# A gated linear recurrence by quotients of running products, with the weights converted beside the first feed-forward block

## The chip, the cores and the metric

The kernel runs on one core of a Trainium2 chip. The metric is the device time in microseconds of one execution. A profile of one execution stands beside the times; its span runs from the first to the last instruction.

## The reference

Four batches, 8 heads, 768 tokens, heads of 48 channels; then a bilinear feed-forward layer over the 3072 tokens of 8 x 48 = 384 channels, with 1536 inner columns. The three weights come as float64, all other inputs as float32.

```python
f = 1 / (1 + exp(-f_logit))                       # (B, H, S, D), f_logit = 2 + 0.5 * normal
for t in range(S):
    state = f[t, :, None] * state + k[t, :, None] * v[t, None, :]
    y[t] = q[t] @ state
x = y as (B*S, H*D)                               # 3072 x 384
out = ((x @ w_a) * (x @ w_b)) @ w_out             # 384 -> 1536 -> 384
```

## The kernel before

Two heads share a tile of 128 partitions, one from partition 0, one from partition 64, with channels on partitions and tokens along the free axis. There are 16 such pairs, each with all 768 tokens. `attention` (L135) treats a pair in chunks of 128 tokens. Inside a chunk the scores are made level by level: at level m, a power of two, key and query lie in neighbouring blocks of m tokens, q scaled by the product of f from the start of its block, k by the product to the end of its own. The fine levels (diagonal, 1, 2, 4, 8, 16) are 48 x 32 x 32 matmuls (L175), masked on DVE (L188) and summed on POOL (L195 to L203). Between levels `grow` (L166) multiplies q and k in place on DVE; POOL makes the block products (L156). Levels 32 (L224) and 64 (L243) follow, then transposes of k (L261), the chunks' gains (L271), the chain of states on DVE (L285), and the output (L295 within a chunk, L304 from the state). The six fine levels alone are 288 small matmuls of a pair.

Finished rows of y go by DMA from SP's queue into `xT` (L319), the feed-forward part's input with channels on partitions. `ffn` (L324) takes a batch in two blocks of 384 tokens. A block has 12 steps of six matmuls 128 x 128 x 384 (L335; first b, then a; ACT copies b at L343, DVE multiplies at L345) and 3 steps of 12 matmuls with `w_out` (L350; ACT copies at L358, SP stores at L360).

The weights are converted from float64 by integer operations (`from_double`, L110 to L131) in 36 pieces of 128 x 384: ACT takes the absolute value of the high words (L122), POOL clamps (L123), DVE does four steps (L124 to L127), POOL adds the low words' part (L128), DVE puts the sign back (L129). Three raw buffers hold pieces that are being loaded.

The order of the work is written out: `manual_schedule` keeps each engine's instructions in program order. Two pairs run in turns, and between their groups stands the feed-forward part of the batch before, or, during batch 0, the weights:

```python
            behind = ffn(b - 1) if b else weights()
            n_behind = NB * (NFT + NTG) if b else 3 * NKT * DFF // PIECE
```

So no feed-forward matmul comes ahead of the end of batch 0's recurrence, and the last batch's feed-forward part runs alone.

Of the kernel before, what the change touches and what calls it, by code (L numbers as in the profile page):

```python
# [9 lines left out]
FP32 = mybir.dt.float32  # L10
U32 = mybir.dt.uint32
# [8 lines left out]
R = 64  # partitions that a head takes in a tile of two heads  # L20
# [10 lines left out]
def kernel(  # L31
    ctx: ExitStack,
    tc: tile.TileContext,
    q: bass.AP,  # (B, H, D, S)
    k: bass.AP,  # (B, H, D, S)
    f_logit: bass.AP,  # (B, H, D, S)
    v: bass.AP,  # (B, H/2, C, S/C, 2, D)
    masks: bass.AP,  # (128, len(FINE), 32)
    moe_w_a: bass.AP,  # float32, or float64 as uint64
# [4 lines left out]
    nc = tc.nc  # L44
    B, H, D, S = q.shape
    NCH = S // C
    HP = H // 2
    DFF, DM = moe_w_out.shape[0], out.shape[1]
    NKT, NFT = DM // 128, DFF // 128
# [4 lines left out]
    NSET = 4  # L54

    const = ctx.enter_context(tc.tile_pool(name="const", bufs=1))
    sb2 = ctx.enter_context(tc.tile_pool(name="sb2", bufs=2))
    ab_pool = ctx.enter_context(tc.tile_pool(name="ab", bufs=NFT + 2))
    raw_pool = ctx.enter_context(tc.tile_pool(name="raw", bufs=3))
# [3 lines left out]
    def fixed(shape, name):  # L63
        return const.tile(shape, FP32, tag=name, name=name)
# [302 lines left out]
    with tc.manual_schedule():  # L367
        for i in range(NSET):
            clear_set(i)
            load_pair(i)  # L370
            if i == 0:
                nc.sync.dma_start(out=mask, in_=masks)
                make_identity(nc, ident)
# [60 lines left out]
```

## Time and profile before

| | |
|---|---|
| three runs | 1057.3, 1058.38, 1060.23 us; median 1058.38 |
| profiled execution: span | 1053.9 us, 28435 instructions (its own time is given by this span alone) |
| PE, matmul | busy 814.0 us (77%), 13040 instructions |
| PEld, weight load | busy 517.2 us (49%), 13040 |
| DVE | busy 402.9 us (38%), 780 |
| ACT | busy 141.4 us (13%), 269 |
| POOL | busy 266.3 us (25%), 330 |
| mean granted TensorE clock | 0.891 |
| DMA | 44.39 MB, 42055 packets |

PE is TensorE's matmuls, PEld its weight loads, which run beside them; DVE is VectorE, ACT ScalarE, POOL GpSimd, SP the engine whose queue issues most DMAs. A row of groups gives line, engine, operation, output <- inputs, shapes, count | busy time, mean ns of one | idle time of that engine just before them and what ended it. A row of the timeline gives start and length in us. A row of busy time by stretch gives the stretch, its length, busy time and instructions of PE, PEld, DVE, ACT and POOL, the granted clock, the DMA engines' share and GB/s. An f32 matmul appears as two instructions.

### The profile page before, as it was taken

To read this page: it belongs to the slowest core of one execution; us is meant where nothing else is said; L and a number is where in the kernel's file an instruction comes from. 1 tells how busy PE (TensorE), PEld (TensorE's weight loads), DVE (VectorE), ACT (ScalarE), POOL (GpSimd) and SP (SyncE) were. 2 spreads that over 40 slices of the span, in tenths; PEclk is the share of its full clock that TensorE was granted. 3 is DMA by queue.
4 is the path that set the end of the run, shared out by engine and by line. 5 is a ranking of instruction groups with operands and counts; after the bars stand their busy time and mean duration, and the time that the engine had idled before them with its cause. 6 is when DMAs were issued, how large, how long until landed. Compare 5 with 4: busy or idle time off the path is not lost.

```text
span 1053.9 us, 28435 instructions
## 1 busy us (share of the span) xinstructions
PE 814.0 (77%) x13040; PEld 517.2 (49%) x13040; DVE 402.9 (38%) x780; ACT 141.4 (13%) x269; POOL 266.3 (25%) x330
## 2 busy tenths in 40 slices
PE   2113512125399989997999899979997999999998
PEld 2112312123265656654665566655565656555554
DVE  4556446564445224522452245234523442010110
ACT  1102110120002110201020102010211121110110
POOL 6354144531414031403140314031403140000000
PEclk9999555555599989998999899989998999999999
DMA  9322342224200230032003200320000000000000
GB/s 183 100 58 72 87 117 63 62 75 92 53 3 2 64 74 3 2 72 66 3 2 72 66 3 2 72 66 2 3 20 28 3 2 19 27 1 14 9 1 22
DMA packets 42055, 44.39 MB, mean 42 GB/s; under 512 B 27984, under 2 KB 31184, under 8 KB 41936
## 3 DMA queue, kind: packets, MB, share of 16 engines
q1 hardware_dynamic: 41936, 42.58, 16.7%
q8 instruction: 102, 1.67, 0.7%
q14 instruction: 17, 0.14, 0.0%
HBM read 33.13 MB, written 4.72 MB: 36 GB/s over the span
## 4 chain that ended last, share of the span: by engine, by line
PE 71%; DVE 11%; POOL 8%; issue 4%; DMA 3%; SPq 2%; ACT 1%; DVEq 0%; ACTq 0%; POOLq 0%
PE f L335 38%; PE f L350 18%; PE a L175 6%; PE a L304 3%; PE a L295 3%; POOL h L128 3%; POOL at L203 2%; DVE qg L147 1%; DVE r L127 1%; DVE k_in L166 1%; DVE tmp L188 1%; DVE r L125 1%; DMA raw<-in_moe_w_out_dram 1%; SPq L92 1%; DMA raw<-in_moe_w_a_dram 1%
## 5 line engine op out<-in xcount | busy, mean ns | idle before, releaser
L335 PE MATMUL f<-xT,w_b 128*128 128x384 f32 x576 | 220.2, 521 | 0.0
L335 PE MATMUL f<-xT,w_a 128*128 128x384 f32 x576 | 203.6, 490 | 0.0
L175 PE MATMUL a<-qg,k_in 48*32 48x32 f32 x7680 | 86.9, 216 | 142.4 <-DVE qg L147 63.2
L350 PE MATMUL f<-w_out,ab 128*128 128x384 f32 x576 | 189.7, 487 | 0.0
L345 DVE TENSOR_TENSOR ab<-f,b_sb 128x384 f32<-128x384 f32 x96 | 53.4, 556 | 317.7 <-PE f L335 317.7
L175 PEld LDWEIGHTS a<-qg,k_in 48*32 48x32 f32 x7680 | 77.9, 117 | 166.5 <-issue 70.5
L335 PEld LDWEIGHTS f<-xT,w_a 128*128 128x128 f32 x576 | 111.5, 194 | 79.3 <-issue 5.5
L350 PEld LDWEIGHTS f<-w_out,ab 128*128 128x128 f32 x576 | 108.0, 190 | 71.9
L335 PEld LDWEIGHTS f<-xT,w_b 128*128 128x128 f32 x576 | 108.6, 199 | 64.3 <-issue 7.8
L343 ACT COPY b_sb<-f 128x384 f32<-128x384 f32 x96 | 45.9, 478 | 372.4 <-PE f L335 372.4
L166 DVE TENSOR_TENSOR k_in<-k_in,tots 128x384 f32<-128x384 f32 x96 | 85.4, 890 | 0.0
L197 POOL TENSOR_TENSOR acc<-acc,tmp 128x384 f32<-128x384 f32 x32 | 38.7, 1211 | 176.3 <-DVE tmp L188 175.7
L156 POOL TENSOR_TENSOR tots<-f_in 128x384 f32<-128x384 f32 x16 | 18.1, 1129 | 252.9 <-ACT f_in L145 252.9
L203 POOL TENSOR_TENSOR at<-acc,tmp 32x384 f32<-32x384 f32 x64 | 71.8, 1122 | 4.1
L147 DVE TENSOR_TENSOR qg<-q_in,f_in 128x768 f32<-128x768 f32 x16 | 18.4, 1149 | 140.0 <-ACT f_in L145 139.8
L188 DVE TENSOR_TENSOR tmp<-a,mask 128x384 f32<-128x384 f32 x96 | 48.9, 550 | 42.0 <-PE a L175 40.4
L166 DVE TENSOR_TENSOR qg<-qg,tots 128x384 f32<-128x384 f32 x96 | 61.2, 637 | 9.1 <-PE a L175 7.7
L128 POOL TENSOR_TENSOR h<-h,r 128x384 f32<-128x384 f32 x36 | 35.7, 992 | 95.3 <-DVE r L127 95.3
L295 PE MATMUL a<-at,v_in 128*64 128x128 f32 x384 | 44.6, 331 | 19.3 <-DVE state L285 19.3
L304 PE MATMUL a<-qg,state 128*128 128x128 f32 x160 | 45.2, 370 | 0.0
L122 ACT ACTIVATE h<-raw 128x384 f32<-128x384 f32 x36 | 19.7, 551 | 149.7 <-DMA raw<-in_moe_w_a_dram 51.4
L295 PEld LDWEIGHTS a<-at,v_in 128*64 128x64 f32 x384 | 22.2, 154 | 35.9 <-issue 30.1
(45 smaller groups left out, 504.2 us busy)
## 6 DMA issues: line engine op xcount, KB each, us to landing
f_in<-in_f_logit_dram SPq DMA_DIRECT2D x32, 144.0 KB, 2.8
q_in<-in_q_dram SPq DMA_DIRECT2D x32, 144.0 KB, 3.5
k_in<-in_k_dram SPq DMA_DIRECT2D x32, 144.0 KB, 3.7
v_in<-in_v_dram SPq DMA_DIRECT2D x16, 288.0 KB, 4.8
raw<-in_moe_w_b_dram SPq DMA_DIRECT2D x12, 384.0 KB, 3.1
raw<-in_moe_w_a_dram SPq DMA_DIRECT2D x12, 384.0 KB, 3.2
raw<-in_moe_w_out_dram SPq DMA_DIRECT2D x12, 384.0 KB, 3.0
out_dram<-o_sb SPq DMA_DIRECT2D x24, 192.0 KB, 1.9
```

What stands on the lines that cost most here:

```text
L128: nc.gpsimd.tensor_tensor(h, h, r, ALU.add)
L166: nc.vector.tensor_tensor(x, x, sp[:, :, e:e + 1].broadcast_to((128, nb, m)), ALU.mult)
L175: nc.tensor.matmul(ps[32 * p:32 * p + 32, par, o:o + 32], lhsT=kg[r, s0:s0 + 32], rhs=qs[r, s0:s0 + 32], start=True, stop=True,)
L188: nc.vector.tensor_tensor(tmp[:, par * NCH:(par + 1) * NCH].rearrange("s c l t -> s c (l t)"), ps[:, par, 0:NCH * 64].rearrange("s (c x) - ...
L197: nc.gpsimd.tensor_tensor(acc, acc, tmp[:, :, 0], ALU.add)
L203: nc.gpsimd.tensor_tensor(at[r].rearrange("s two c t -> s (two c) t")[:, :, r], acc[r], tmp[r, :, 1], ALU.add)
L295: nc.tensor.matmul(o[R * par:R * par + R], lhsT=vv[:, c, par], rhs=at[:, par, c], start=True, stop=c == 0, skip_group_check=True,)
L304: nc.tensor.matmul(o, lhsT=st[:, c - 1], rhs=qg[:, c * C:c * C + C], start=False, stop=True, skip_group_check=True)
L335: nc.tensor.matmul(ps[nm], lhsT=w[:, kt, ft * 128:ft * 128 + 128], rhs=x[:, kt, cols], start=kt == 0, stop=kt == NKT - 1,)
L343: nc.scalar.copy(b_sb, ps["b"])
L345: nc.vector.tensor_tensor(ab[ft], ps["a"], b_sb, ALU.mult)
L350: nc.tensor.matmul(o, lhsT=ab[ft][:, tg * 128:tg * 128 + 128], rhs=w_out[:, ft], start=ft == 0, stop=ft == NFT - 1,)
```

## The change

The recurrence now goes in units of 384 tokens of four heads (two head pairs side by side in the free axis): 16 units, two for each of the eight feed-forward blocks. With P_t the running product of f inside a unit, the score of s and t is (q_t P_t) . (k_s / P_s), so no levels are needed. P starts from e^34, which keeps P and 1/P within float32 as long as the product over a unit is not below e^-68.

- `front`: two sigmoids give f and nearly 1/f; POOL and a third ACT pass make a correction factor; two scans on DVE give P, two more 1/P; q and k are multiplied by them in place.
- `scores`: 24 matmuls 48 x 64 x 64 inside sub-blocks of 64 tokens, masked by one DVE operation. `turn`: 6 transposes of k and an ACT copy. `gains`: 24 matmuls (20 in the last half), then the states are running sums on DVE, with one multiplication by P at the unit's end. `within` and `across`: 24 matmuls each into one accumulator, three ACT copies, five DMAs to `xT` from ACT's queue (they were SP's).
- PSUM: one two-bank tile for scores, transposes and gains, one for the output, four banks for the feed-forward part.
- Weights: 36 pieces in the order in which the first block needs them, converted during the start and the first block. `from_double` takes the sign by a Sign activation and puts it back by a product; the absolute value is taken a second time after POOL's sum. ACT has three operations a piece (before one), DVE four (before five), POOL two.
- The order: units 0 and 1 with the first pieces written out by hand; then the parts of each later unit's `slot` at given steps of the feed-forward blocks. In block 0 the conversions stand ahead of each step, and the `w_out` part runs over all three token groups at once.
- A check: DVE notes for each channel and unit whether the product stayed above e^-68; before the last block the notes are summed into one flag. At the end each engine reads the flag, and only if it is set the old scheme runs again over everything (`by_levels`, the old code without the weights).

```diff
+K_EXP = 75.0
+MIDDLE = 34.0
+DECAY_MAX = 68.0
...
+    make_identity(nc, ident)
+    with ExitStack() as pools:
+        by_quotients(pools, tc, q, k, f_logit, v, moe_w_a, moe_w_b, moe_w_out, out, ident, weights, bad)
+    again = nc.values_load(bad[0:1, 0:1], min_val=0, max_val=1, skip_runtime_bounds_check_because="it is a comparison's result")
+    with tc.If(again > 0), ExitStack() as pools:
+        by_levels(pools, tc, q, k, f_logit, v, masks, out, ident, weights)
...
+    def pieces():
+        for ft in range(NFT):
+            for dst, src in ((w_b, moe_w_b), (w_a, moe_w_a)):
+                cols = slice(ft * 128, ft * 128 + 128)
+                yield dst[:, :, cols], src.rearrange("(kt p) c -> p kt c", p=128)[:, :, cols], (NKT, 128)
+        for ft in range(NFT):
+            yield w_out[:, ft:ft + 1], moe_w_out[ft * 128:ft * 128 + 128].unsqueeze(1), (1, DM)
+    todo, raws = list(pieces()), []
+    def load_weights():
+        if len(raws) < len(todo):
+            dst, src, shape = todo[len(raws)]
+            raw = dst
+            if src.dtype != FP32:
+                raw = raw_pool.tile([128, *shape], mybir.dt.uint64, tag="raw", name="raw")
+            nc.sync.dma_start(out=raw, in_=src)
+            raws.append(raw)
+    def convert(n):
+        while done[0] < min(n, len(todo)):
+            dst, src, shape = todo[done[0]]
+            if src.dtype != FP32:
+                from_double(dst, raws[done[0]], shape)
+            done[0] += 1
+            load_weights()
+    def from_double(dst, raw, shape):
+        words = raw.bitcast(U32).rearrange("p k (n two) -> p (k n) two", two=2)
+        lo, hi = words[:, :, 0], words[:, :, 1]
+        h, r, sign = (sb2.tile([128, PIECE], FP32, tag=n, name=n) for n in ("h", "r", "sign"))
+        hu, ru = h.bitcast(U32), r.bitcast(U32)
+        nc.scalar.activation(h, hi.bitcast(FP32), AF.Abs)
+        nc.scalar.activation(sign, hi.bitcast(FP32), AF.Sign)
+        nc.gpsimd.tensor_scalar(h, h, HI_MAX, HI_MIN, ALU.min, ALU.max)
+        nc.vector.tensor_scalar(hu, hu, 3, 0x40000000, ALU.logical_shift_left, ALU.bitwise_xor)
+        nc.vector.tensor_scalar(ru, hu, 0xFF800000, None, ALU.bitwise_and)
+        nc.vector.scalar_tensor_tensor(out=r, in0=lo, scalar=2.0**-52, in1=r, op0=ALU.mult, op1=ALU.mult)
+        nc.gpsimd.tensor_tensor(h, h, r, ALU.add)
+        nc.scalar.activation(h, h, AF.Abs)
+        h, sign = (x.rearrange("p (k n) -> p k n", k=shape[0]) for x in (h, sign))
+        nc.vector.tensor_tensor(dst, h, sign, ALU.mult)
...
+    def front(u):
+        t = sets[u % NSET]
+        x = halves(t["f"])
+        f, inv, fix = (sb2.tile([128, 2 * BLK], FP32, tag=n, name=n) for n in ("f", "inv", "fix"))
+        nc.scalar.activation(f, x, AF.Sigmoid)
+        nc.scalar.activation(inv, x, AF.Sigmoid, bias=less, scale=-1.0)
+        nc.gpsimd.tensor_scalar(inv, inv, math.exp(K_EXP), 1.0, ALU.mult, ALU.add)
+        nc.gpsimd.tensor_tensor(fix, f, inv, ALU.mult)
+        nc.scalar.activation(fix, fix, AF.Identity, bias=two, scale=-1.0)
+        yield
+        for n in range(2):
+            c = slice(n * BLK, n * BLK + BLK)
+            nc.vector.tensor_tensor_scan(x[:, c], f[:, c], zeros, math.exp(MIDDLE), ALU.mult, ALU.add)
+        nc.vector.tensor_scalar(held[:, u], t["f"][:, :, BLK - 1], math.exp(MIDDLE - DECAY_MAX), None, ALU.is_ge)
+        nc.vector.tensor_tensor(halves(t["q"]), halves(t["q"]), x, ALU.mult)
+        yield
+        for n in range(2):
+            c = slice(n * BLK, n * BLK + BLK)
+            nc.vector.tensor_tensor_scan(inv[:, c], inv[:, c], fix[:, c], math.exp(-MIDDLE), ALU.mult, ALU.mult)
+        nc.vector.tensor_tensor(halves(t["k"]), halves(t["k"]), inv, ALU.mult)
+        live[u] = {}
+        yield
+    ps_x, ps_y = (ps_a.tile([128, 2, 512], FP32, tag=n, name=n) for n in ("ps_x", "ps_y"))
...
+    def scores(u):
+        t = sets[u % NSET]
+        qf, kf = halves(t["q"]), halves(t["k"])
+        ps = ps_x
+        for n, c, o in each():
+            for h in range(2):
+                for p in range(2):
+                    r = slice(R * h, R * h + D)
+                    nc.tensor.matmul(
+                        ps[SUB * p:SUB * p + SUB, h, o:o + SUB],
+                        lhsT=kf[r, tokens(n, c, p)],
+                        rhs=qf[r, tokens(n, c, p)],
+                        start=True,
+                        stop=True,
+                    )
+        at = sb2.tile([128, 2, BLK], FP32, tag="at", name="at")
+        nc.vector.tensor_tensor(
+            at.rearrange("s h (o t) -> s h o t", t=SUB),
+            ps[:, :, 0:BLK].rearrange("s h (o t) -> s h o t", t=SUB),
+            causal.unsqueeze(1).unsqueeze(1).broadcast_to((128, 2, 2 * NC, SUB)),
+            ALU.mult,
+        )
+        live[u]["at"] = at
+    def turn(u):
+        kf = halves(sets[u % NSET]["k"])
+        kT = sb1.tile([128, 2, NC, 128], FP32, tag="kT", name="kT")
+        for n in range(2):
+            for c in range(NC):
+                o = n * BLK + c * C
+                nc.tensor.transpose(ps_x[:, n, c * C:c * C + C], kf[:, o:o + C], ident)
+        nc.scalar.copy(kT.rearrange("s n c x -> s n (c x)"), ps_x[:, :, 0:BLK])
+        live[u]["kT"] = kT
+    def gains(u):
+        _, half, _ = unit(u)
+        t, kT = sets[u % NSET], live[u]["kT"]
+        last = half == NH - 1
+        for n in range(2):
+            for c in range(NC):
+                for p in range(2):
+                    if last and c == NC - 1 and p == 1:
+                        continue
+                    for h in range(2):
+                        r = slice(SUB * p, SUB * p + SUB)
+                        nc.tensor.matmul(
+                            ps_x[R * h:R * h + D, p, (n * NC + c) * D:(n * NC + c) * D + D],
+                            lhsT=kT[r, n, c, R * h:R * h + D],
+                            rhs=t["v"][r, n, c, h * D:h * D + D],
+                            start=True,
+                            stop=True,
+                        )
+        st = sb4.tile([128, NJ, 2, D], FP32, tag="st", name="st")
+        before = live[u - NQ]["st"][NJ] if half else None
+        live[u]["st"] = [before]
+        for j in range(NJ - 1 if last else NJ):
+            c, p = divmod(j, 2)
+            new = ps_x[:, p, 0:2 * NC * D].rearrange("r (n c d) -> r n c d", n=2, c=NC)[:, :, c]
+            if before is None:
+                nc.vector.tensor_copy(st[:, j], new)
+            else:
+                nc.vector.tensor_tensor(st[:, j], before, new, ALU.add)
+            before = st[:, j]
+            live[u]["st"].append(before)
+        if not last:
+            for n in range(2):
+                end = t["f"][:, n, BLK - 1:BLK]
+                nc.vector.tensor_scalar(before[:, n], before[:, n], end, math.exp(-MIDDLE), ALU.mult, ALU.mult)
+    def within(u):
+        t, at = sets[u % NSET], live[u]["at"]
+        for n, c, o in each():
+            for p in range(2):
+                for h in range(2):
+                    r = slice(SUB * p, SUB * p + SUB)
+                    e = R * (p ^ h)
+                    nc.tensor.matmul(
+                        ps_y[e:e + D, p, o:o + SUB],
+                        lhsT=t["v"][r, n, c, h * D:h * D + D],
+                        rhs=at[r, h, o:o + SUB],
+                        start=o == 0,
+                        stop=True,
+                        skip_group_check=True,
+                    )
+    def across(u):
+        b, half, qd = unit(u)
+        qf, st = halves(sets[u % NSET]["q"]), live[u]["st"]
+        for n, c, o in each():
+            for p in range(2):
+                j = 2 * c + p
+                if j == half == 0:
+                    continue
+                for h in range(2):
+                    r, e = slice(R * h, R * h + D), R * (p ^ h)
+                    nc.tensor.matmul(
+                        ps_y[e:e + D, p, o:o + SUB],
+                        lhsT=st[j][r, n],
+                        rhs=qf[r, tokens(n, c, p)],
+                        start=False,
+                        stop=True,
+                        skip_group_check=True,
+                    )
+        y = sb1.tile([128, 2 * NC, 2, SUB], FP32, tag="y", name="y")
+        for p, e, r, rows in ((0, 0, 0, 128), (1, R, 0, R), (1, 0, R, R)):
+            nc.scalar.copy(
+                y[r:r + rows, :, p], ps_y[e:e + rows, p, 0:BLK].rearrange("r (o m) -> r o m", m=SUB)
+            )
+        y = y.rearrange("r (n c) p m -> r n (c p m)", n=2)
+        blk = b * NH + half
+        if qd == 0:
+            xT[blk] = sb2.tile([128, NKT, BLK], FP32, tag="xT", name="xT")
+        for n in range(2):
+            for h in range(2):
+                ch, row, left = (4 * qd + 2 * n + h) * D, R * h, D
+                while left:
+                    kt, p = divmod(ch, 128)
+                    w = min(left, 128 - p)
+                    nc.scalar.dma_start(out=xT[blk][p:p + w, kt], in_=y[row:row + w, n])
+                    ch, row, left = ch + w, row + w, left - w
+        live.pop(u - NQ, None)
+        load_unit(u + NSET)
...
+    def slot(u):
+        nxt = front(u + 1) if u + 1 < NU else iter(())
+        if u > NQ:
+            within(u - 1)
+        if u < NU:
+            scores(u)
+        yield
+        next(nxt, None)
+        yield
+        if u < NU:
+            turn(u)
+        yield
+        next(nxt, None)
+        yield
+        if u > NQ:
+            across(u - 1)
+        if u < NU:
+            gains(u)
+        yield
+        next(nxt, None)
+        yield
+    def check_held():
+        n = NU * 2
+        some = fixedp.tile([128, 1], FP32, tag="some", name="some")
+        nc.vector.reduce_sum(some, held.rearrange("p u j -> p (u j)"), axis=mybir.AxisListType.X)
+        ps = ps_x
+        nc.tensor.matmul(ps[0:1, 0, 0:1], lhsT=some, rhs=ones, start=True, stop=True)
+        nc.vector.tensor_scalar(bad, ps[0:1, 0, 0:1], 128.0 * n, None, ALU.is_lt)
...
+        for _ in range(3):
+            load_weights()
+        fronts = [front(u) for u in range(NQ + 1)]
+        for u in range(NQ):
+            next(fronts[u])
+            next(fronts[u])
+        convert(1)
+        for u in range(NQ):
+            next(fronts[u])
+        for u in range(NQ, NSET):
+            load_unit(u)
+        scores(0)
+        turn(0)
+        convert(2)
+        gains(0)
+        next(fronts[2])
+        within(0)
+        scores(1)
+        turn(1)
+        across(0)
+        next(fronts[2])
+        convert(4)
+        gains(1)
+        next(fronts[2])
+        within(1)
+        slots = {s: slot(s) for s in range(NQ, NU + 1)}
+        next(slots[NQ])
+        next(slots[NQ])
+        next(slots[NQ])
+        across(1)
+        convert(6)
+        queue = []
+        for s in slots:
+            for d in (0, 1, 2.2, 3.4, 4.6, 5.8)[3 if s == NQ else 0:]:
+                queue.append(((s - NQ) * (NFT + NTG) / 2 - 6 + d, s))
+        queue.sort(reverse=True)
+        for blk in range(NBLK):
+            for i in range(10**6):
+                step = blk * (NFT + NTG) + (min(i, NFT) + max(i - NFT, 0) / 4 if blk == 0 else i)
+                while queue and queue[-1][0] <= step:
+                    next(slots[queue.pop()[1]], None)
+                if i == 0:
+                    part = ffn(blk)
+                if blk == 0:
+                    convert(min(2 * i + 6, 2 * NFT) if i < NFT - 2 else NFT + i + 4)
+                if next(part, "end") == "end":
+                    break
+            if blk == NBLK - 2:
+                check_held()
...
-            behind = ffn(b - 1) if b else weights()
-            n_behind = NB * (NFT + NTG) if b else 3 * NKT * DFF // PIECE
+            behind = ffn(b - 1) if b else iter(())
+            n_behind = NB * (NFT + NTG)
```

More of the change, by code (lines that the diff above doesn't have):

```diff
@@ L1 @@
+import math
 import struct
@@ L10 @@
 FP32 = mybir.dt.float32
+I32 = mybir.dt.int32
 U32 = mybir.dt.uint32
@@ L44, with fixed @@
     nc = tc.nc
+    DFF, DM = moe_w_out.shape[0], out.shape[1]
+    NKT, NFT = DM // 128, DFF // 128
+    const = ctx.enter_context(tc.tile_pool(name="const", bufs=1))
+    def fixed(shape, name, dtype=FP32):
+        return const.tile(shape, dtype, tag=name, name=name)
+    ident = fixed([128, 128], "ident")
+    w_a = fixed([128, NKT, DFF], "w_a")
+    w_b = fixed([128, NKT, DFF], "w_b")
+    w_out = fixed([128, NFT, DM], "w_out")
+    bad = fixed([1, 1], "bad", I32)
+    weights = (w_a, w_b, w_out)
@@ L45, with by_levels @@
+def by_levels(ctx, tc, q, k, f_logit, v, masks, out, ident, weights):
+    nc = tc.nc
     B, H, D, S = q.shape
@@ L47 @@
     HP = H // 2
-    DFF, DM = moe_w_out.shape[0], out.shape[1]
-    NKT, NFT = DM // 128, DFF // 128
+    w_a, w_b, w_out = weights
+    NKT, NFT, DM = w_a.shape[1], w_out.shape[1], out.shape[1]
     NB = S // BLK
@@ L74 @@
     st_tiles = [fixed([128, NCH - 1, 128], f"state{i}") for i in range(2)]
-    ident = fixed([128, 128], "ident")
     mask = fixed([128, len(FINE), 32], "mask")
-    w_a = fixed([128, NKT, DFF], "w_a")
-    w_b = fixed([128, NKT, DFF], "w_b")
-    w_out = fixed([128, NFT, DM], "w_out")
     def clear_set(i):
```

156 lines of the change are left out of this document (124 added, 32 removed).

## The prediction

> **What bounds the kernel now.** I read the profile page first, then busy time by stretch, the chain of waits and the timeline of single stretches.
>
> ```profile
> span 1053.9 us, 28435 instructions
> ...
> 0.00:271.00 271.00, 78.05 (x2924) 61.73 (x2924) 146.08 (x307) 36.45 (x66) 110.70 (x149) 0.70 0.39 93
> 271.00:911.00 640.00, 596.52 (x9685) 373.68 (x9686) 243.40 (x449) 90.11 (x173) 155.58 (x182) 0.95 0.12 28
> 911.00:1054.00 143.00, 139.40 (x433) 81.81 (x431) 13.38 (x24) 14.82 (x31) 0.00 (x0) 1.00 0.03 10
> ...
> 283.43 5.71 PE f L335 x12
> ...
> 592.80 2.23 issue
> ...
> 911.08 46.44 PE f L335 x144
> 957.52 23.22 PE f L350 x72
> ```
>
> There are three stages. For 271 us PE is busy 78 us: the recurrence of batch 0 and the weights pass through short steps of DVE, POOL and ACT, and no feed-forward matmul can run. For 640 us PE is busy 597 us: six feed-forward blocks, and twelve pairs of heads between them. The last 143 us are two blocks alone at full clock. A block is 46.44 + 23.22 = 69.66 us, an instruction of 384 columns 46.44 / 144 = 322.5 ns. Eight blocks are 557 us, which the change doesn't touch. Twelve pairs cost PE 640 - 6 x 69.66 = 222 us, 18.5 us each. So two things can shrink: the 271 us ahead of the first block, and those 222 us.
>
> **The change, part by part.** A unit of 384 tokens of four heads is as much work as a pair was; there are 16.
>
> *PE work of a unit.* In place of 6 x 48 fine score matmuls and the levels above come scores, within, across and gains, 24 matmuls each (48 instructions, as an f32 matmul is two), and 6 transposes. The nearest rows:
>
> ```profile
> 426.41 0.62 PE L224 MATMUL a<-qg,k_in 48*32 48x32 f32 x48
> 426.96 2.20 PE L335 MATMUL f<-xT,w_b 128*128 128x384 f32 x6
> ...
> 332.44 1.54 PE a L243 x48
> 333.99 4.07 PE f L335 x12
> ...
> 441.17 0.71 PE L261 MATMUL a<-ident,k_in 128*128 128x128 f32 x5
> ...
> 441.71 2.10 PE L335 MATMUL f<-xT,w_b 128*128 128x384 f32 x6
> ```
>
> A feed-forward step behind a group of small matmuls takes 4.07 us instead of 12 x 0.3225 = 3.87, so each visit costs 0.2 us more, plus some 0.1 going in. L224 (32 columns, four corners of the array) takes 426.96 - 426.41 + 0.2 - 0.3 = 0.45 us for 48, 9 ns each; L243 (64 columns, two parts of the array) 1.55 + 0.2 - 0.3 = 1.45 us, 30 ns each. The new groups have 64 columns (gains 48) in four corners. Streamed four at a time 64 columns need 322.5 x 64 / 384 / 4 = 13 ns. Ends 14 and 30 ns; I take 20, as L224, whose corners are alike, needed 9 where the same reckoning gives 7. A slot has two visits of 96 instructions, 2 x (0.3 + 1.92), and the transposes, 0.66 (441.71 - 441.17 = 0.54 for five): 5.1 us, ends 4.0 and 7.1, against 18.5.
> [...]
>
> *The conversion of a weight piece.* This decides the first block. Before:
>
> ```profile
> 30.09 0.56 ACT L122 ACTIVATE h<-raw 128x384 f32<-128x384 f32 x1 [17.53 <-DMA raw<-in_moe_w_b_dram]
> 30.73 0.51 POOL L123 TENSOR_SCALAR h<-h 128x384 f32<-128x384 f32 x1 [4.70 <-ACT h L122]
> 31.04 0.55 ACT L122 ACTIVATE h<-raw 128x384 f32<-128x384 f32 x1 [0.39 <-DMA raw<-in_moe_w_b_dram]
> 31.27 0.36 DVE L124 TENSOR_SCALAR h<-h 128x384 uint32<-128x384 uint32 x1 [4.82 <-POOL h L123]
> 31.67 0.36 DVE L125 TENSOR_SCALAR r<-h 128x384 uint32<-128x384 uint32 x1
> 32.06 0.36 DVE L126 TENSOR_SCALAR h<-h 128x384 uint32<-128x384 uint32 x1
> 32.34 0.55 DVE L127 SCALAR_TENSOR_TENSOR r<-raw,r 128x384 f32<-128x384 uint32 x1
> 32.97 0.99 POOL L128 TENSOR_TENSOR h<-h,r 128x384 f32<-128x384 f32 x1 [1.73 <-DVE r L127]
> 34.00 0.85 DVE L129 SCALAR_TENSOR_TENSOR w_b<-raw,h 128x384 uint32<-128x384 uint32 x1 [1.11 <-POOL h L128]
> ...
> L197 POOL TENSOR_TENSOR acc<-acc,tmp 128x384 f32<-128x384 f32 x32 | 38.7, 1211 | 176.3 <-DVE tmp L188 175.7
> ...
> raw<-in_moe_w_a_dram SPq DMA_DIRECT2D x12, 384.0 KB, 3.2
> ```
>
> ACT takes the next piece at 31.04, while the first is still on its way: it has one instruction a piece. The change gives it three: Abs, Sign, and a second Abs that waits for POOL's sum. Each engine follows the order written, so the next piece's first Abs stands behind this piece's second, and the pieces no longer overlap. The ring: Abs to POOL 30.09 to 30.73 = 0.64; POOL to DVE 0.54; two tensor_scalar and the product, 0.40 + 0.28 + 0.55, and the step to POOL 0.08, = 1.31; POOL's sum and the step back 1.03; Abs again 0.55 (Sign lies beside POOL and DVE): 4.05 us a piece. Without the steps between engines it is 3.7; with POOL's sum at 1.21, as its additions at L197 take, and longer steps 4.6. A loaded piece waits two pieces, 8 us, against 3.2 us to landing, so the loads are hidden.
>
> *The other operations of a unit.*
>
> ```profile
> L145 ACT ACTIVATE f_in<-f_in 128x768 f32<-128x768 f32 x16 | 12.7, 838 | 4.4 <-DMA f_in<-in_f_logit_dram 4.4
> L147 DVE TENSOR_TENSOR qg<-q_in,f_in 128x768 f32<-128x768 f32 x16 | 18.4, 1149 | 140.0 <-ACT f_in L145 139.8
> L188 DVE TENSOR_TENSOR tmp<-a,mask 128x384 f32<-128x384 f32 x96 | 48.9, 550 | 42.0 <-PE a L175 40.4
> L285 DVE SCALAR_TENSOR_TENSOR state<-state,tots,a 64x48 f32<-64x48 f32 x128 | 33.7, 263 | 4.1
> L343 ACT COPY b_sb<-f 128x384 f32<-128x384 f32 x96 | 45.9, 478 | 372.4 <-PE f L335 372.4
> L308 ACT COPY y<-a 128x768 f32<-128x768 f32 x16 | 12.7, 796 | 63.8 <-PE a L304 63.8
> L345 DVE TENSOR_TENSOR ab<-f,b_sb 128x384 f32<-128x384 f32 x96 | 53.4, 556 | 317.7 <-PE f L335 317.7
> L83 POOL MEMSET k_in<- 128x768 f32 x4 | 3.0, 738 | 0.3 <-POOLq L424 0.3
> ...
> xT<-y SPq DMA_DIRECT2D x24, 144.0 KB, 2.8
> ...
> 1.69 0.87 SPq L92 DMA_DIRECT2D f_in<-in_f_logit_dram  x2
> ...
> 5.20 1.28 ACT L145 ACT_TABLE_LOAD   x1 [5.20 <-DMA f_in<-in_f_logit_dram]
> ```
>
> No scan is in the trace. It has 384 steps, so a product of 384 elements (0.56) bounds it below, one of 768 (1.15) above; I take 0.9, nearer the upper end, as a step needs the one before it. [...]
> The first front stage: two sigmoids and a third pass on ACT at 0.84, and POOL between them for a scalar pass of 768 (2 x 0.51) and a product (2 x 0.99) with its steps, 3.2: it holds ACT for 5.7 us. The second and third: two scans and a product on DVE, 2.9 us each. Mask 1.1, states 6 x 0.26 and two small ones 1.8, turning copy 0.8, output copies 3 x 0.48 = 1.4. The five moves of y to xT go from SP's queue to ACT's; ACT has no row for an issue, SP's is 0.87 / 2 = 0.43, so 2.2 us of ACT (ends 0.3 and 2.2). Behind them on ACT stand the next conversion and the copies of b. On SP they no longer hold up the weight loads.
>
> *Up to the first feed-forward matmul.* It needs units 0 and 1 whole. f lands at 5.5 (5.2 before; one POOL clear more ahead). Sigmoids to 7.2, POOL (eight clears of 0.7 and the small ones end near 7.7) to 10.7, ACT 11.6; unit 1 the same, 17.2. Piece 1, 4.05 and its last product 0.6: 21.9. Only now, by the order of DVE, the third stages of both units: 27.5. Mask 28.6, transposes at half clock 30.0, copy 30.9, piece 2 35.5, states 37.3. Scores of unit 1 38.8, mask 39.9, transposes 41.3, across 42.6, copies 44.1, moves issued 46.3, pieces 3 and 4 55.0, states 56.8, third stage of unit 2 59.7, scores 61.2, mask 62.3, transposes 63.7, across of unit 1 65.0, copies 66.4, issue 68.6, landed about 71: the first matmul, where before it came at 283.43. ACT goes on with pieces 5 and 6 until 76.7. Ends 58 (fast scans, cheap issues) and 85.
>
> *The first block.* It waits for the ring: 30 pieces x 4.05 = 121.5. Between them in the same order stand twelve copies of b, 5.8; the rest of unit 2's slot on DVE (2.9 + 1.8 + 2.9), 7; and two slots' work where it lies on the ring: first stages 11.4, three DVE stages less the 0.56 of slack beside ACT 7, masks 1, turning copies 1.6, outputs 7.2, in all 28 (ends 15 and 43). 76.7 + 162.3 = 239, and the last product and three matmuls 2.5: the block ends at 242. PE's own 70 + 13 us lie beneath that.
>
> *Afterwards.* Seven blocks, 7 x 69.66 = 487.6; 11.5 slots x 5.1 = 58.7 (ends 46 and 82). DVE has about 12 us and ACT 10 us of a unit for 35 us of matmuls, so their waits are covered; if that cover goes, PE waits for scans or for ACT's copies of b.
>
> ```profile
> 1050.48 0.48 ACT L358 COPY o_sb<-f 128x384 f32<-128x384 f32 x1 [7.31 <-PE f L350]
> 1050.99 0.33 SPq L360 DMA_DIRECT2D out_dram<-o_sb  x1
> ```
>
> *The end.* 1053.9 - 1050.4 = 3.5 us as before. Then each engine reads the flag and jumps over the general path, for which no row stands: it can't be a gain, and two transfers of some 2 us, one for the flag and one for code, are what I take, 4 (ends 0 and 12). The flag itself is ready a block earlier.
>
> Sum: 242 + 487.6 + 58.7 + 3.5 + 4 = 796 us of span. The page gives the profiled execution as its span, 1053.9; the runs' median 1058.38 is 4.5 more. So 800 us.
>
> **The rivals.**
> *The pieces overlap after all.* If the first block went at PE's rate, it would end at 71 + 83 = 154 and the time would be 800 - 88 = 712. For it: ACT ran ahead before (31.04). Against: the second Abs. It decides from a piece below about 2.2 us.
> *PE waits in the middle blocks.* scores, transposes and gains share one PSUM tile, so each waits for DVE or ACT to have read the last. 5 us of waiting a slot gives 800 + 58 = 858. For it: PE had waits of some 2 us between pairs before (the "issue" piece at 592.80). Against: two feed-forward steps, 8 us, lie between the visits.
> [...]
> *The general path runs.* It does if in any channel the product of f over 384 tokens is below e^-68. Then the level scheme and all eight blocks follow, some 930 us (1054 less an estimate of 120 for the weights, half of the first stage): 1730 us, slower than before. From the inputs, f = sigmoid(2 + 0.5 x normal) has a mean of -ln f near 0.14, so 54 with a spread of 1.3: far from 68.
>
> **How the numbers follow.** Forecast 0.72, overlap 0.13, waits in the middle 0.08, serial loads 0.04, general path 0.03. The forecast's own ends, not all met at once, are 765 and 850. Leaving out overlap, the general path and a tail, the range is 742 to 862. All but the last case are faster; 0.3% is about what can be told from no change here: faster 0.96, same 0.01, slower 0.03.
>
> **What would show it.** The profile after should show 3,456 feed-forward instructions with a mean as before; PE poor until about 240 us and 9 from there on; conversions about 4 us apart in the first block, with ACT's second Abs waiting for POOL; steps of 5 us of small matmuls twice a block; no instruction of the level scheme. It is wrong if the pieces come closer than 3 us, if PE has gaps in the middle blocks, if a scan takes over 1.2 us, or if more than 20 us follow the last matmul.

## The result and the profile after

The changed kernel takes 789.94 us (median of 4 runs, 789.36 to 790.11) against 1058.09 us before: a ratio of 0.7452, 95% interval 0.7434 to 0.7469. The profiled execution took 789.36 us with a span of 787.6 us.

The profile page of the changed kernel, then its busy time by stretch (columns as before: length; PE, PEld, DVE, ACT, POOL; granted clock, DMA share, GB/s):

```profile
span 787.6 us, 11346 instructions
...
PE   0235555554867999999999999999999999999996
...
0.00:71.00 71.00, 17.48 (x473) 15.46 (x474) 40.48 (x62) 21.61 (x33) 26.96 (x37) 0.85 0.54 135
71.00:247.00 176.00, 103.18 (x612) 57.36 (x608) 86.57 (x181) 60.92 (x126) 54.74 (x68) 0.81 0.30 87
247.00:710.00 463.00, 463.00 (x3475) 282.47 (x3473) 122.69 (x225) 93.08 (x168) 26.40 (x20) 1.00 0.14 38
```

The row of PE shows it at once: with holes up to the thirteenth slice, full from then on. In the third stretch PE is busy for every microsecond of the 463; in the second, the first feed-forward block, no engine is busy for more than 103 of 176 us. That is how a chain that passes from engine to engine looks.

The chain of waits of the changed kernel (start, length, what), where the first block ends, one slot, and the end:

```profile
242.74 1.00 POOL h L179
244.94 2.20 PE f L386 x6
247.14 3.87 PE f L366 x12
251.01 0.82 PE ps_y L306 x48
251.83 0.70 PE ps_x L235 x48
252.53 7.94 PE f L366 x24
260.47 0.66 PE ps_x L257 x6
...
710.41 46.64 PE f L366 x144
757.05 23.23 PE f L386 x72
```

Up to 244.94 the chain runs through POOL's sum of the weight pieces and its neighbours; from there to the end it is PE alone. From 247.14 to 780.28 are 533.1 us, of which seven blocks take 7 x 69.66 = 487.6. The 11.5 slots share 45.5 us, 4.0 us each, where a pair had cost 18.5.

The span is 266 us shorter, and that comes from three places. The work between feed-forward blocks fell from 222 to 45.5 us: 176. The first feed-forward matmuls can start at 71 instead of 283, but the first block then ends at 247, 177 us more than a block alone takes, against 271 before: 94. And the end grew by 4.

### The profile page after: what moved, and what is told of

Its sections match the earlier page's. It is cut to its first block, busy times and chain, and to the rows that moved or that the text cites. A ratio compares the mean times of both kernels' runs of the same rounds, so it can differ in the third digit from the quotient of the medians.

```text
span 787.6 us, 11346 instructions
## 1 busy us (share of the span) xinstructions
PE 653.9 (83%) x4770; PEld 396.3 (50%) x4770; DVE 256.6 (33%) x480; ACT 183.3 (23%) x341; POOL 108.1 (14%) x125
## 4 chain that ended last, share of the span: by engine, by line
PE 69%; DVE 10%; POOL 9%; ACT 6%; issue 4%; ACTq 1%; DMA 0%; POOLq 0%
PE f L366 42%; PE f L386 21%; POOL h L179 5%; DVE r L178 3%; POOL h L175 2%; ACT h L173 2%; DVE r L177 2%; DVE h L176 2%; PE ps_y L326 2%; PE ps_x L257 2%; PE ps_x L235 1%; POOL fix L199 1%; PE ps_y L306 1%; ACT h L180 1%; DVE inv L210 1%
## 5 line engine op out<-in xcount | busy, mean ns | idle before, releaser
L235 PE MATMUL ps_x<-q_in,k_in 48*64 48x64 f32 x768 | 18.0, 248 | 68.4 <-DMA k_in<-in_k_dram 27.1
L235 PEld LDWEIGHTS ps_x<-q_in,k_in 48*64 48x64 f32 x768 | 16.2, 161 | 68.9 <-issue 57.3
L396 ACT COPY o_sb<-f 128x384 f32<-128x384 f32 x24 | 11.5, 480 | 166.9 <-PE f L386 158.6
L180 ACT ACTIVATE h<-h 128x384 f32<-128x384 f32 x36 | 18.9, 525 | 110.0 <-POOL h L179 110.0
L204 DVE TENSOR_TENSOR_SCAN f_in<-f,zeros 128x384 f32<-128x384 f32 x32 | 30.8, 1003 | 3.5 <-ACT inv L196 3.5
L175 POOL TENSOR_SCALAR h<-h 128x384 f32<-128x384 f32 x36 | 19.7, 548 | 82.1 <-ACT h L173 82.1
L199 POOL TENSOR_TENSOR fix<-f,inv 128x768 f32<-128x768 f32 x16 | 30.7, 1917 | 1.3
L210 DVE TENSOR_TENSOR_SCAN inv<-inv,fix 128x384 f32<-128x384 f32 x32 | 30.6, 999 | 0.0
L289 DVE TENSOR_TENSOR st<-st,ps_x 128x96 f32<-128x96 f32 x80 | 20.3, 254 | 21.7 <-PE ps_x L273 19.2
L337 ACT COPY y<-ps_y 64x384 f32<-64x384 f32 (+1 forms) x48 | 22.9, 476 | 17.9 <-PE ps_y L326 17.4
L200 ACT ACTIVATE fix<-fix,two 128x768 f32<-128x768 f32 x16 | 15.0, 939 | 48.7 <-POOL fix L199 48.7
```

Of the source, the lines that this page charges most:

```text
L175: nc.gpsimd.tensor_scalar(h, h, HI_MAX, HI_MIN, ALU.min, ALU.max)
L180: nc.scalar.activation(h, h, AF.Abs)
L199: nc.gpsimd.tensor_tensor(fix, f, inv, ALU.mult)
L204: nc.vector.tensor_tensor_scan(x[:, c], f[:, c], zeros, math.exp(MIDDLE), ALU.mult, ALU.add)
L210: nc.vector.tensor_tensor_scan(inv[:, c], inv[:, c], fix[:, c], math.exp(-MIDDLE), ALU.mult, ALU.mult)
L235: nc.tensor.matmul(ps[SUB * p:SUB * p + SUB, h, o:o + SUB], lhsT=kf[r, tokens(n, c, p)], rhs=qf[r, tokens(n, c, p)], start=True, stop=True,)
```

## The experiments

Times are medians; each ratio is to the kernel before, run beside it on the same chip. `e3_one_pass`, `e7_half_columns` and `e12_half_weights` leave out work that the output needs and measure time alone.

| kernel | us | ratio, 95% interval |
|---|---|---|
| the change | 789.94 | 0.7452, 0.7434 to 0.7469 |
| e1_lag1 | 744.95 | 0.7035, 0.7007 to 0.7063 |
| e2_lag2 | 729.40 | 0.6885, 0.6858 to 0.6913 |
| e3_one_pass | 677.51 | 0.6396, 0.6372 to 0.6419 |
| e4_early | 827.91 | 0.7813, 0.7784 to 0.7842 |
| e5_sp_moves | 777.79 | 0.7361, 0.7346 to 0.7375 |
| e6_no_check | 786.06 | 0.7432, 0.7419 to 0.7445 |
| e7_half_columns | 784.21 | 0.7416, 0.7403 to 0.7429 |
| e8_old_form | 762.80 | 0.7214, 0.7200 to 0.7227 |
| e9_lag2_sp | 721.62 | 0.6809, 0.6776 to 0.6842 |
| e10_sum_dve | 723.44 | 0.6830, 0.6796 to 0.6865 |
| e11_late_start | 730.13 | 0.6889, 0.6854 to 0.6925 |
| e12_half_weights | 790.73 | 0.7470, 0.7450 to 0.7490 |

My theory was that the first block is paced by the ring of one weight piece, because each engine keeps the written order and ACT's next Abs stands behind this piece's second. The rivals: the loads pace the pieces; DVE and POOL get in each other's way; sheer amount of work.

### The ring, taken apart by order alone

`e1_lag1` issues the second Abs and the last product of a piece behind the next piece's passes (in outline):

```diff
-            from_double(dst, raws[done[0]], shape)     # all nine passes of piece n
+            begin(n + 1)      # Abs, Sign, POOL pass, DVE x3, POOL sum of piece n + 1
+            finish(n)         # second Abs and product of piece n
```

> The same operations for each weight piece, in another order: the second Abs and the last product of a piece are issued behind the next piece's passes up to POOL's sum. Ring theory (the first block is paced by one piece's chain, because ACT's next Abs stands behind this piece's second Abs): the loop that is left is POOL's scalar pass, three DVE passes and POOL's sum, 0.54 + 1.31 + 1.03 = 2.9 us a piece in place of 4.05, so 30 pieces x 1.15 = 34 us less, 755 us. Rival, the loads through three raw buffers pace the pieces: nothing changes, 790 us. Rival, POOL and DVE get in each other's way: their passes grow longer and the pieces stay near 4 us, above 780 us.

`e2_lag2` makes three stages of it: DVE's passes and POOL's sum of piece n + 1 are issued behind the first Abs, Sign and POOL pass of piece n + 2, and the second Abs and product of piece n behind those; h, r and sign get three buffers.

> Three stages instead of two: a piece's DVE passes and POOL sum are issued behind the next piece's first Abs and POOL pass, and its second Abs and product behind the stage after that; three buffers for h, r and sign. Ring theory: the pieces go at the pace of the busiest engine, DVE, some 1.9 us; 30 x 2.15 = 64 us less, 726 us, as long as PE's own work in the first block (some 80 us from 71) doesn't show first, which would be at 694. Loads as the pace: 790 us. Contention of POOL and DVE: no better than the kernel with two stages.

744.95 and 729.40 us. The timeline of the changed kernel first, one piece and the start of the next (Sign and one pass of DVE left out):

```profile
49.38 0.54 ACT L173 ACTIVATE h<-raw 128x384 f32<-128x384 f32 x1 [2.74 <-DMA xT<-y]
50.01 0.51 POOL L175 TENSOR_SCALAR h<-h 128x384 f32<-128x384 f32 x1 [8.54 <-ACT h L173]
50.56 0.36 DVE L176 TENSOR_SCALAR h<-h 128x384 uint32<-128x384 uint32 x1 [5.71 <-POOL h L175]
...
51.34 0.56 DVE L178 SCALAR_TENSOR_TENSOR r<-raw,r 128x384 f32<-128x384 uint32 x1
51.99 0.99 POOL L179 TENSOR_TENSOR h<-h,r 128x384 f32<-128x384 f32 x1 [1.47 <-DVE r L178]
53.01 0.52 ACT L180 ACTIVATE h<-h 128x384 f32<-128x384 f32 x1 [2.65 <-POOL h L179]
53.44 0.54 ACT L173 ACTIVATE h<-raw 128x384 f32<-128x384 f32 x1
```

ACT waits 2.65 us for POOL's sum, and the next piece begins at 53.44, 4.06 us after 49.38. POOL's sums in the timeline of `e1_lag1`, with one product of DVE:

```profile
90.91 0.55 DVE L192 TENSOR_TENSOR w_a<-h,sign 128x384 f32<-128x384 f32 x1
91.08 1.25 POOL L188 TENSOR_TENSOR h<-h,r 128x384 f32<-128x384 f32 x1 [1.47 <-DVE r L187]
...
94.27 1.25 POOL L188 TENSOR_TENSOR h<-h,r 128x384 f32<-128x384 f32 x1 [1.47 <-DVE r L187]
```

The pieces now come 3.19 us apart with the same operations and the same three raw buffers. The forecast of 2.9 had POOL's sum at 0.99; beside DVE's product of the piece before it takes 1.25. Yet the kernel gained 45 us where 34 were expected. From piece 5 to piece 36 are 31 steps: 31 x 0.87 = 27 us are the pieces, for 16 us the other work between them adds less (24 us instead of 40), and 2 us come at the start. Copies of b and masks, for one, now lie beside the loop: two pieces with a copy of b and a mask beside them have products 102.22 - 97.41 = 4.81 us apart in the changed kernel, 94.10 - 90.91 = 3.19 here. That loads pace the pieces is refuted for this loop; that POOL and DVE disturb each other is true, but a quarter of a microsecond of it.

`e2_lag2` came out at 729.40 where 726 was expected. DVE is the limit, as I gave it: it is busy 104.45 of 115 us. But its passes are longer than I took them. POOL's sum and a DVE pass in its timeline, and its first block by stretch:

```profile
89.52 1.25 POOL L189 TENSOR_TENSOR h<-h,r 128x384 f32<-128x384 f32 x1 [0.49 <-DVE r L188]
89.83 1.16 DVE L186 TENSOR_SCALAR h<-h 128x384 uint32<-128x384 uint32 x1
...
71.00:186.00 115.00, 89.63 (x601) 52.99 (x602) 104.45 (x175) 55.79 (x117) 60.02 (x64) 0.88 0.42 119
```

A DVE pass of 0.36 us takes 1.16 when it starts under POOL's sum, and ends 0.2 us after it. So the pieces stay at 2.7 us instead of 1.9, and the total is near the forecast by luck: the pieces give 31 x 1.34 = some 41 us and not 64, the work between them gives 14 us and the start 6, which I had not counted. With the loop this short, two loads of weight pieces stand in the chain of waits, 3.85 and 3.44 us, where the changed kernel's chain has none.

### No conversion, and all conversions first

In outline:

```diff
-    from_double: nine passes
+    from_double: nc.scalar.activation(dst, hi.bitcast(FP32), AF.Abs)
```

> Leaves the conversion out: one ACT pass takes the high words' absolute values as the weights, the loads stay. Ring theory: the first block runs at PE's pace, 70 + 2.5 slots x 4 = 80 us, and about 17 us of conversions go from the start: 790 - 96 - 17 = 677 us, up to 700 if ACT's first stages of the units hold it up. Loads as the pace: 14 MB through three buffers as now, near 780 us.

677.51 us. From 57 us to the end of the first block PE waits once, for 0.30 us, and the second block begins at 136.19 (in the changed kernel at 247.14); the loads, all 14 MB of them through the same three buffers, hold PE up nowhere:

```profile
111.41 11.77 PE L375 MATMUL f<-w_out,ab 128*128 128x384 f32 x36
123.12 0.89 PE L315 MATMUL ps_y<-q_in,st 48*48 48x64 f32 x48
...
124.47 11.88 PE L375 MATMUL f<-w_out,ab 128*128 128x384 f32 x36
136.19 2.10 PE L355 MATMUL f<-xT,w_b 128*128 128x384 f32 x6
```

So 112 us of the 790 are the conversions (less the one pass of ACT that is left), and hardly more than that can be had from them.

```diff
         across(1)
-        convert(6)
+        convert(len(todo))
```

> Converts all pieces ahead of the first block, where they stood before the change, in place of beside it. Ring theory: 30 pieces x 4.05 = 121 us from 83 on, until 204, with nothing beside it but two steps of matmuls; then the first block in some 80 us, until 283 in place of 247: 826 us. If converting beside the block saved nothing, 790 us; if all of the first block's own work was hidden under the conversions, 870 us.

827.91 us, 38 us more. This is what "weights converted later" is worth with this ring: some 38 us, of the 70 us of matmuls that lie beside it. The chain of waits shows the first block behind the conversions, which end at 204.6 (204 expected); unit 2's scans come between:

```profile
204.62 1.73 DVE f_in L204 x2
...
213.13 9.21 PE f L366 x24
```

### One operation on ACT instead of three

`e8_old_form` keeps the new order and takes the old operations: one Abs on ACT, five passes on DVE, the sign by bits.

```diff
-        nc.scalar.activation(sign, hi.bitcast(FP32), AF.Sign)
...
-        nc.scalar.activation(h, h, AF.Abs)
-        nc.vector.tensor_tensor(dst, h, sign, ALU.mult)
+        nc.vector.tensor_scalar(hu, hu, 0x40000000, None, ALU.bitwise_xor)
...
+        nc.vector.scalar_tensor_tensor(out=dst, in0=hi, scalar=0x80000000, in1=hu, ...)
```

> The weights by the old operations in the new order: one ACT operation a piece, five on DVE, two on POOL. Ring theory: ACT runs ahead again, and DVE in order is the pace: 0.40 + 0.39 + 0.28 + 0.55 + 0.08, POOL's sum 1.03, the last product 0.56 to 0.85: 3.3 to 3.6 us a piece, so 13 to 22 us less, 768 to 777 us, although DVE does more work. If the amount of work on DVE set the pace, the time would rise, above 790 us.

762.80 us: 27 us faster than the change, though DVE has a pass more. DVE's last pass of two neighbouring pieces:

```profile
109.63 0.85 DVE L181 SCALAR_TENSOR_TENSOR w_b<-raw,h 128x384 uint32<-128x384 uint32 x1 [1.11 <-POOL h L179]
...
113.12 0.85 DVE L181 SCALAR_TENSOR_TENSOR w_a<-raw,h 128x384 uint32<-128x384 uint32 x1 [1.11 <-POOL h L179]
```

3.49 us a piece, inside the forecast of 3.3 to 3.6; 30 x 0.57 = 17 us. The other 10 us I had not counted, so the time lies below the range I gave: by the trace the work between the pieces adds 34 us instead of 40, and the start is 2 us shorter. ACT is off the loop, and with it its copies of b, of k and of y; that this is the reason was not tried by itself. Taken alone, the new form of the conversion in place of the old one costs 27 us in this order.

### The moves of y, the check

```diff
-                    nc.scalar.dma_start(out=xT[blk][p:p + w, kt], in_=y[row:row + w, n])
+                    nc.sync.dma_start(out=xT[blk][p:p + w, kt], in_=y[row:row + w, n])
```

> Undoes one part: the five moves of y to xT are issued from SP's queue again. In the changed kernel they hold ACT for 3.1 us a unit. If ACT's order paces start and first block, four units' moves lie on it (units 0 to 3): 4 x 3.1 = 12 us less, 778 us. Rival: on SP the moves wait for ACT's copies with the weight loads behind them, and the loads come late: 790 us or more.

777.79 us, as the theory had it: 12 us for four units. The timeline of the changed kernel shows ACT's queue taken for 3.10 us and the next Abs behind it:

```profile
150.08 3.10 ACTq L351 DMA_DIRECT2D xT<-y  x5
153.28 0.56 ACT L173 ACTIVATE h<-raw 128x384 f32<-128x384 f32 x1 [2.73 <-DMA k_in<-in_k_dram]
```

The wait is put down to a load of k, which this Abs does not read; the row above it is the cause.

`e6_no_check` leaves out the check:

```diff
-    again = nc.values_load(bad[0:1, 0:1], ...)
-    with tc.If(again > 0), ExitStack() as pools:
-        by_levels(...)
```

> Leaves out the flag, its read at the end, the jump and the general path's code. The end after the last matmul is 7.3 us in the changed kernel against 3.5 before: 4 us less, 786 us. If the jump costs nothing, 790 us; if the code of the general path also cost loading time along the way, below 784 us.

786.06 us: 3.9 us less. Its span ends 784.4 - 780.84 = 3.6 us after the last matmul, the changed kernel's 7.3 us.

### What sets the small matmuls

> Streams 32 instead of 64 columns in scores, within and across, with the same weights loaded (the other half of the outputs is left out). The groups take 14.6 to 17 ns an instruction at 64 columns; streaming through four corners would be 13. If streaming sets it, an instruction falls to the 9 ns that the old kernel's 32-column groups showed: 3 x 48 x 6 ns = 0.9 us a slot, 11.5 slots, 10 us less, 780 us. If the loads of the weights set it, 790 us.

> The counterpart of the kernel with half the columns: scores, within and across load half as many weight columns (32 of 64, 24 of 48) and stream all 64 (the other outputs are left out). With half the columns streamed, scores stayed at 0.81 us for 48 instructions and within fell from 0.71 to 0.56. If loading sets scores alone, it falls towards 0.5 here and the others stay: 0.3 us a slot, 3 to 4 us less, 786 us. If loading sets all three, 0.9 us a slot, 780 us. If neither, 790 us.

784.21 us with half the columns, 790.73 with half the weight columns. The same slot in the chains of waits, first with half the columns, then with half the weights:

```profile
249.98 0.67 PE ps_y L306 x48
250.65 0.70 PE ps_x L235 x48
...
251.56 0.80 PE ps_y L306 x48
252.36 0.67 PE ps_x L235 x48
```

In the changed kernel they are 0.82 and 0.70. So `within` falls by 0.15 us with half the columns and hardly at all with half the weights; `scores` hardly moves with either. (The expectation's 0.71 and 0.81 are the same two groups from start to start in the timeline: there `within` is 0.71, 0.56 with half the columns, 0.69 with half the weights, and `scores` 0.81, 0.81 and 0.78.) So columns set a part of `within`, and halving the loads alone lowers nothing. That does not clear the loads: in the changed kernel they run beside the matmuls (PEld busy 396.3 us and PE 653.9 in a span of 787.6), and if the longer of the two sets the pace, which no run shows, halving one of two equal ones changes nothing either. `scores` has 64 of both. No run here halves both; the nearest is the kernel before, whose L224 has 32 of both and takes 426.96 - 426.41 = 0.55 us from start to start, against 0.81. It stays open. In the total, half the columns are worth 0.5 to 0.7%, half the weights nothing.

### Combinations

`e9_lag2_sp` puts `e2_lag2` and `e5_sp_moves` together, `e10_sum_dve` also moves POOL's sum to DVE, `e11_late_start` is `e9_lag2_sp` without the conversions inside the first two units' chain:

```diff
# e10
-        nc.gpsimd.tensor_tensor(h, h, r, ALU.add)
+        nc.vector.tensor_tensor(h, h, r, ALU.add)
# e11
-        convert(1)
-        convert(2)
-        convert(4)
```

> The three-stage conversions together with the moves of y on SP's queue. In the three-stage kernel DVE is busy 104 of the 115 us of the first block, so the moves no longer lie on what paces it; only the two at the start do: 2 x 3.1 = 6 us less than 729, 723 us. If ACT's order still paced the block, 12 us less, 717 us.

> As the kernel before it in this call, with POOL's sum of a piece moved to DVE. Under three stages DVE's first scalar pass took 0.72 us beside that sum, 0.36 in the changed kernel, and its product 0.71 instead of 0.56. If the two engines hold each other up, five undisturbed DVE passes (0.36 + 0.36 + 0.56 + 0.55 + 0.56 = 2.4 us) are no longer than four disturbed ones (2.6), and it is 3 to 8 us faster than its neighbour, about 717 us. If they don't, DVE has 30 x 0.5 us more to do and it is 15 us slower, about 738 us.

> As the first kernel of this call, without the conversions inside the chain of the first two units: all pieces come behind unit 1's output. The first feed-forward matmul can come some 12 us earlier. If DVE's amount of work up to the end of the first block sets the time, the same passes are only done later, and it is within 3 us of the first kernel, about 722 us; if the start's chain sets it, 10 to 15 us less, about 710 us.

721.62 us is the fastest kernel here that computes everything: 68 us less than the change. It lies between both expectations of its own, nearer to the one by which only the start's moves count.

`e10_sum_dve` gives 723.44 us, which meets neither expectation: not faster, but a fifth pass cost 1.8 us instead of 15. DVE's rows of the stretch 71 to 180 us, first of `e9_lag2_sp`, then of `e10_sum_dve`:

```profile
L186 DVE TENSOR_SCALAR h<-h 128x384 uint32<-128x384 uint32 x29 | 20.4, 704 | 0.0
L187 DVE TENSOR_SCALAR r<-h 128x384 uint32<-128x384 uint32 x29 | 14.4, 496 | 1.0
...
L189 DVE TENSOR_TENSOR h<-h,r 128x384 f32<-128x384 f32 x29 | 19.2, 661 | 1.0
L187 DVE TENSOR_SCALAR r<-h 128x384 uint32<-128x384 uint32 x29 | 11.7, 402 | 1.0
L186 DVE TENSOR_SCALAR h<-h 128x384 uint32<-128x384 uint32 x29 | 10.2, 352 | 0.0
```

Without POOL's sum the two scalar passes are back at 0.35 and 0.40 us: 13 us of DVE were lost to the overlap there. With some shorter products (into `w_out` 0.55 us each instead of 0.60) and scans (two of f in the chain of waits 1.99 us instead of 2.33, two others 2.00 instead of 2.80) that nearly pays for the fifth pass, 19.2 us: in all DVE is busy 99.0 us of this stretch instead of 97.2.

`e11_late_start` gives 730.13 us, slower than both expectations. The first matmuls start at 57.76 instead of 63.47, but the second block at 188.80 instead of 180.56. DVE did 144.8 us of work up to 180 us against 149.6: waits in the start's chain that the conversions had filled stayed empty, and that work came later. The chain of waits shows another hole, behind the first matmuls:

```profile
58.48 6.22 DMA raw<-in_moe_w_a_dram
66.20 1.09 DVE w_a L193
```

The fourth piece's load needs a raw buffer that the first piece has left, and on SP's queue it stands behind five moves of y and seven loads of a unit; it is issued at 58.48 and lands at 64.7; by the timeline PE waits 5.62 us for that piece's product, until 67.35. I had weighed the start's chain against DVE's amount of work, and neither the idle time nor this load. How the 8.5 us divide between the two was not tried: a run that issues this load ahead of the moves would show it.

## Why the prediction was right, point by point

The forecast was 800 us, the time is 789.94.

- *First matmul at 71.* Two instructions came at 71.22; the others of that step waited until 75.31 for the last moves to land, and ACT, which I had free for piece 5 at 68.6, began it at 74.55. Piece 6 was done at 83.4 instead of 77.3. Of the 6 us, some 0.9 are the second sigmoid's constant, which POOL clears behind the sets; some 3 are POOL's passes and DVE's scans where they meet (in each of the first two units ACT waits 4.05 us for POOL where 3.2 were reckoned, and two scans take 3.35 us instead of 1.8); about 1 is the moves, whose issues take 3.1 us of ACT's queue, so that the next Abs begins 2.7 us behind the copies instead of 2.2, twice; the rest is spread. Rows of the changed kernel's timeline:

```profile
7.21 0.94 ACT L196 ACTIVATE inv<-f_in,less 128x768 f32<-128x768 f32 x1 [0.99 <-POOL less L442]
8.23 1.53 POOL L198 TENSOR_SCALAR inv<-inv 128x768 f32<-128x768 f32 x1 [0.19 <-ACT inv L196]
60.17 3.35 DVE L210 TENSOR_TENSOR_SCAN inv<-inv,fix 128x384 f32<-128x384 f32 x2
```

- *The first block.* From there to its end 247.0 - 83.4 = 163.6 us, where 242 - 77.3 = 164.7 were reckoned. A piece took 4.06 us against 4.05, with two of its steps off by 0.12 in opposite directions: DVE's part is 51.99 - 50.56 = 1.43 instead of 1.31, and the second Abs holds ACT 53.44 - 53.01 = 0.43 instead of 0.55. The work between the pieces added 40 us against 40.8; its largest parts are two first stages, 11.4 as reckoned, and two outputs, 8.8 instead of 7.2. `e1_lag1`, `e8_old_form` and `e3_one_pass` show that it was this ring and its cause, the order on ACT: 45, 27 and 112 us went when the order or the form was changed or the conversion left out.
- *The slots.* The term that was mis-sized most: 5.1 us forecast, 4.0 measured, 45.5 instead of 58.7 us in all. An instruction of the four-cornered groups took 14 to 17 ns; I had 20, in the middle of 14 and 30, and the row of the old 64-column groups should have counted less than that of L224. To serial loads the prediction gives 0.04; what they would cost a slot, no run shows. A whole slot, loads included, took 4.0 us, and half the weights changed nothing (790.73 us against 789.94).
- *Waits in the middle blocks.* None: PE is busy 463.00 of 463 us. The shared PSUM tile was read in time.
- *The scan.* Taken as 0.9 us; the rows of the changed kernel:

```profile
L204 DVE TENSOR_TENSOR_SCAN f_in<-f,zeros 128x384 f32<-128x384 f32 x32 | 30.8, 1003 | 3.5 <-ACT inv L196 3.5
87.63 1.80 DVE L210 TENSOR_TENSOR_SCAN inv<-inv,fix 128x384 f32<-128x384 f32 x2
```

  Two undisturbed ones take 1.80 us, 0.90 each, as taken; the mean of 1.0 holds those that ran beside POOL. There two took 3.35 us (the row at 60.17, beside POOL's product of 2.56 us from 60.15), over the 1.2 us that the prediction named as a sign of being wrong; it made the start longer and left the middle blocks as they were.
- *The end.* 7.3 us against 7.5; by `e6_no_check` the check is 7.3 - 3.6 = 3.7 us of it, 4 forecast. That the 4 are two transfers of some 2 us was my assumption; no run shows them. The general path did not run: the trace has none of its instructions.
- *The count.* The page has 3 x 576 = 1,728 feed-forward instructions, as 8 blocks of 144 + 72 give; the 3,456 of the prediction counted them twice. Their means, 518, 491 and 495 ns, are within 2% of those before.
- *Around the span.* I added 4.5 us, the difference of one execution's span and the median of others; here the profiled execution's time is 789.36 - 787.6 = 1.8 us more than its span.

The misses add up: +5 at the first block's end, -13 for the slots, -3 around the span: 800 - 11 = 789. So errors of opposite sign met, and the total looks a little better than its parts.

What the prediction did not see is what the change gives away. In the same order, the old form of the conversion is 27 us faster, three stages 61 us, and with the moves on SP 68 us.

## What to carry to other kernels

When engines keep the written order, write down for each engine what stands behind an operation that waits: an operation given to an idle engine can cost more than its length if it closes a ring through that engine. Here the second Abs takes 0.52 us, and issuing it and the last product later took 4.06 - 3.19 = 0.87 us off a piece (`e1_lag1`). A stretch in which no engine is busy for most of the time can be the sign of such a ring; here the busiest worked 103 of 176 us. Issuing the second half of one piece behind the first half of the next opened it without any change of the operations. Once it is open, look for what is then the limit before moving more: here it was DVE (busy 104.45 of 115 us in `e2_lag2`), with single loads beginning to show (3.85 and 3.44 us), and clearing the conversions out of the start left DVE idle there (busy 45.49 instead of 52.38 of the first 71 us), brought a late load of 6.22 us into the open and made the kernel slower (730.13 us instead of 721.62).

## What the runs showed of the hardware that I had not expected

DVE and POOL hold each other up. A DVE scalar pass of 0.36 us took 1.16 when it began 0.3 us into POOL's sum, and over the stretch from 71 to 180 us its mean was 0.70 us with POOL's sum (`e9_lag2_sp`) and 0.35 without (`e10_sum_dve`). POOL's sum took 1.25 us instead of 0.99 when a DVE product ran beside it. At the start of the changed kernel POOL's scalar pass of 768 took 1.53 us beside the scans, later 0.83. The pass of 1.16 us ended 0.2 us after POOL's sum did, where an undisturbed one takes 0.36 in all. By what the two engines hold each other up, no run shows.

Small matmuls in four corners of the array took 14 to 17 ns an instruction by the chain of waits; neither half the columns nor half the weights alone brought one clearly below 14.
